# A loop over pairs of steps, with one written order for each engine, in a kernel of attention and two feed-forward layers

## The chip, the cores and the metric

One Trainium2 chip, one of its cores. The metric is the device time of one execution in microseconds (us); lower is better. The engines are PE (TensorE matmul; PEld is its weight load), DVE (VectorE), ACT (ScalarE), POOL (GpSimd) and SP (SyncE, which issues the DMAs). They run side by side, each through its own list of instructions in order, and wait for each other by semaphores.

## The reference

12,480 tokens of width 128 go through attention over 49 agents and two feed-forward layers of width 2,048:

```python
def _attn_ref(q, k, v, agents):
    a2k = sm(agents, k)                 # softmax of scaled scores
    agent_v = a2k @ v                   # 49 x 128
    q2a = sm(q, agents)                 # 12480 x 49
    return q2a @ agent_v

def _moe_ref(x, w_in, w_out):
    h = x @ w_in
    g = np.where(h >= 1, h, np.where(h <= -1, 0, (h + 1) ** 2 / 4))
    return g @ w_out

def _moe2_ref(x, w_in, w_out, s, b):
    r = np.maximum(x @ w_in, 0)
    return (s * (r * r) + b) @ w_out
```

## The kernel before

A prologue (up to some 66 us) sums keys and values into `agent_v`, turns the float64 weights into pairs of fp32r tiles (`h` for the high part, `l` for the rest), and folds `agent_v @ w_in` of the first layer into `awh` and `awl` (49 rows for the high part of the probabilities, 49 for the low, in 128 partitions).

After it the tokens are taken in 25 blocks: one of 256, 23 of 512, one of 448. A block has `JP` = 8 steps; a step is 256 of the 2,048 hidden columns, two chunks of 128, so there are `NS` = 200 steps. Step `n` of the first layer and step `m = n - 11` of the second stand side by side. The parts of a step, with the letters by which the text names them (capital for the first layer, small for the second):

- H(n), four matmuls (L581): two chunks, each with `awh` and `awl`, into a PSUM tile of two banks. h(m) (L581 too) has six: the layer's input is a pair `yh`, `yl`. These tiles, and those of the scores and the transposition, share three buffers (tag `h`); the text calls one of them a buffer.
- R(n), relu by ACT (L597), S(n), square by ACT (L603), M(n), the cap by DVE (L607), which reads the PSUM tile last and so frees it; c(n), the cast to `gh` by DVE (L618); L(n), the rest `gl` by DVE (L623). Second layer: r(m) (L599), which frees the tile; t(m), the square (L603); the cast by ACT (G, L616) or DVE (C, L618) after the pattern PAT2, by DVE alone in the last TL = 11 steps; l(m) (L623).
- O(n), six matmuls (L665) into `y`: for each chunk `wh x gh`, `wl x gh`, `wh x gl`. So the third is the first to read `gl`. o(m) is the same into `o`. O and o come two steps after their H and h.
- At a block's end yh (Y, ACT, L684) and yl (y, DVE, L687) read `y`, and Z (DVE, L691) reads `o` and stores the output.
- The probabilities of a later block: scores (q, L161), a copy by ACT (Q, L168), then ten small operations, the fillers (maximum, subtraction, Exp by ACT at L182, sum, reciprocal, product, two casts on DVE), of which `fill` takes the next at set places; then a transposition (p, L204) and its copy by ACT (P, L209).

The first 14 steps are written out in a string (`RAMP`). From step 14 on a loop over steps (L721 to L758) records the instructions: on PE in the order of `POR`, and on the other engines in that of `ORD`, one list of tokens for ACT and DVE together. The order of recording is the order on each engine. `x`, `gh` and `gl` live in rings of XB, GR and GR buffers for each layer, all 4.

Of the kernel before, what the change touches and what calls it, by code (L numbers as in the profile page):

```python
# [8 lines left out]
F32 = mybir.dt.float32  # L9
F32R = mybir.dt.float32r  # L10
# [8 lines left out]
def kernel(  # L19
# [17 lines left out]
    nc = tc.nc  # L37
    P = 128
# [37 lines left out]
    )  # L78
    WORD = "A0 A2 A1 B0 B1 C0 C1 D0 D1".split()
    PIECE = {"A0": (0, 512), "A2": (512, 512)}  # L80
    POR = "H1 QS QT O1 H2 O2".split()
    NR, ORD = 14, (
        "R1 T2 S1 Q Y G2 R2 C2 L1 F M1 y L2 F Z G1 c1"
    ).split()
    QS, QT, DX = {1: 6, 2: 7, 3: 6, 4: 4}, {2: 6, 3: 5, 4: 3}, 1
    MASK_H = 0x7FFFFE00
    WBIAS = -8.0 * 896 * 2 ** 20
    TB = 512
# [49 lines left out]

    q_t = {}
    qs_t = {}  # L140
    pt_t = {}

    def subs(t):
        w = blocks[t][1]
# [52 lines left out]
    def q_transpose(t):  # L197
        if t >= NB:
            return
        fill(len(fillers), True)  # L200
        w = blocks[t][1]
        tp = ps_h(f"tp{t}")[:, 0, :]
        for i, c0 in enumerate(subs(t)):
            nc.tensor.matmul(  # L204
                out=tp[:, c0:c0 + P], lhsT=ptok[t % NPT][:, i, :], rhs=ident_r,
                start=True, stop=True,
            )
        pt_t[t] = ptp.tile([P, TB], F32R, tag="pt", name=f"pt{t}")
# [489 lines left out]
    def ramp():  # L698
        steps = {}

        def first_q(k):
            ops = q_scores(k)
            steps[k] = [q_evac, *ops[:3], *ops[4:]]

        does = {
            "H": lambda n: H(1, n), "R": lambda n: relu(1, n), "S": lambda n: square(1, n), "M": cap,
            "g": lambda n: hi(1, n, GH(1, n) == "1"), "L": lambda n: lo(1, n), "O": lambda n: O(1, n),
            "h": lambda n: H(2, n), "r": lambda n: relu(2, n), "s": lambda n: square(2, n),
            "G": lambda n: hi(2, n, GH(2, n) == "1"), "l": lambda n: lo(2, n), "o": lambda n: O(2, n),
            "Y": lambda: evac(1, "h"), "y": lambda: evac(1, "l"),  # L710
            "u": load_q, "q": first_q, "p": q_transpose, "P": lambda n: q_evac(), "z": lambda k, i: steps[k][i](),
        }
        for token in RAMP.split():
            does[token[0]](*[int(x) for x in token[1:].split(".") if x])

    with tc.manual_schedule():
        prologue()
        late = ctx.enter_context(tc.tile_pool(name="late", bufs=1))
        ramp()
        fillers.append(lambda: nc.vector.tensor_scalar_mul(bcol, bcol, b_sb[:, 0:1]))  # L720
        for n in range(NR, NS + D + D2):  # L721
            t, j = divmod(n, JP)
            m = n - D
            a1, a2, b2 = n < NS, 0 <= m < NS, 0 <= m - 1 < NS
            b1 = 0 <= n - 1 < NS
            room[0] = 2 if n < 4 * JP else 4
            if j == 0:
                load_q(t + 2)
            for c in POR:
                if c == "H1" and a1: H(1, n)  # L730
                if c == "H2" and a2: H(2, m)
                if c == "O1" and 0 <= n - D1 < NS: O(1, n - D1)
                if c == "O2" and 0 <= m - D2 < NS: O(2, m - D2)
                if c == "QS" and j == QS.get(t, 3): fillers.extend(q_scores(t + 2))
                if c == "QT" and t > 1 and j == QT.get(t, 1): q_transpose(t + 1)
            if m == NS:
                last_step(False)
            b2 = 0 <= m - 1 < NS - 1
            a2 = 0 <= m < NS - 1
            for c in ORD:  # L740
                if c == "T2" and b2: square(2, m - 1)
                if c == "Q": q_evac()
                if c == "Y": evac(1, "h")
                if c == "y": evac(1, "l")
                if c == "Z": evac(2, "")
                if c == "G2" and b2: hi(2, m - 1, True)
                if c == "G1" and a1: hi(1, n, True)
                if c == "R1" and a1: relu(1, n)
                if c == "S1" and a1: square(1, n)
                if c == "R2" and a2: relu(2, m)  # L750
                if c == "M1" and a1: cap(n)
                if c == "c1" and a1: hi(1, n, False)
                if c == "C2" and b2: hi(2, m - 1, False)
                if c == "L1" and b1: lo(1, n - 1)
                if c == "L2" and b2: lo(2, m - 1)
                if c == "F": fill()
            if m == NS - 1:
                last_step(True)  # L758


# [33 lines left out]
```

## Time and profile before

| what | us |
|---|---|
| median of three runs (lowest, highest) | 1114.33 (1113.85, 1114.42) |
| profiled execution, its own time | 1113.61 |
| its span, first to last instruction | 1111.7 |
| PE busy | 1090.9 |
| DVE busy | 983.5 |
| ACT busy | 971.2 |

The profile follows one execution. "Busy" counts an engine's instructions; a PE that is always busy still shows its real pace only in the distance from one matmul to the next, since matmuls overlap. A row of a timeline has its start, its duration, engine, line, operation, output and inputs, and in brackets the idle time before it with what ended it. The `h` rows of both layers look alike (L581): those from `pt` are H, those from `yh` and `yl` are h.

### The profile page before, as it was taken

What the parts mean: (1) busy time and instruction counts of PE and PEld (TensorE: products, weight loads), DVE (VectorE), ACT (ScalarE), POOL (GpSimd) and SP (SyncE); (2) the same over time, 40 slices, a digit from 0 to 9 for tenths busy, and PEclk for the clock granted to TensorE, in tenths of its full rate; (3) what the DMA queues carried; (4) which work ended last, traced back from release to release, by engine and by line L of the source; (5) the groups of instructions that cost most, each with busy time, mean ns of one, the idle gap of its engine ahead of it and who ended that gap; (6) DMA issues with size and microseconds to landing.
All of it is one profiled execution on the core that took longest, in us unless ns stands there. A gap on an engine that the chain in (4) does not pass through costs nothing.

```text
span 1111.7 us, 13231 instructions
## 1 busy us (share of the span) xinstructions
PE 1090.9 (98%) x5050; PEld 879.6 (79%) x5050; DVE 983.5 (88%) x1194; ACT 971.2 (87%) x1132; POOL 0.8 (0%) x7
## 2 busy tenths in 40 slices
PE   7889999999999999999999999999999999999998
PEld 3677788888888888888888888888888888888887
DVE  8889988989889889889889899889889898898886
ACT  6889888888988988998898998998999889889886
POOL 0000000000000000000000000000000000000000
PEclk9999999999999999999999999999999999999999
DMA  9910000000000000000000000000000000000000
GB/s 352 394 58 5 15 1 20 20 1 19 19 2 19 9 11 20 0 19 20 1 19 19 1 19 19 1 20 19 1 20 20 1 19 19 1 10 10 1 10 18
DMA packets 16271, 34.82 MB, mean 31 GB/s; under 512 B 1808, under 2 KB 6736, under 8 KB 15696
## 3 DMA queue, kind: packets, MB, share of 16 engines
q1 hardware_dynamic: 16208, 33.98, 8.7%
q8 instruction: 40, 0.66, 0.2%
q14 instruction: 23, 0.19, 0.1%
HBM read 27.58 MB, written 6.39 MB: 31 GB/s over the span
## 4 chain that ended last, share of the span: by engine, by line
PE 91%; DVE 5%; ACT 1%; DMA 1%; issue 1%; SPq 0%; DVEq 0%
PE h L581 40%; PE o L665 24%; PE y L665 24%; PE qs L161 2%; DVE x L607 1%; DMA k<-in_kT 1%; PE tp L204 1%; DVE gl L623 1%; PE av L436 1%; DVE mxs L393 1%; DVE gh L618 0%; DVE wt L278 0%; ACT wt L268 0%; PE st L419 0%; DVE wu L286 0%
## 5 line engine op out<-in xcount | busy, mean ns | idle before, releaser
L623 DVE TENSOR_TENSOR gl<-x,gh 128x1024 fp32r<-128x1024 f32 (+2 forms) x399 | 475.8, 1193 | 8.0 <-ACT gh L616 0.6
L603 ACT ACTIVATE x<-x 128x1024 f32<-128x1024 f32 (+2 forms) x399 | 392.0, 1033 | 0.5
L597 ACT ACTIVATE x<-h 128x1024 f32<-128x1024 f32 (+2 forms) x200 | 201.1, 1007 | 106.8 <-PE h L581 106.4
L607 DVE SCALAR_TENSOR_TENSOR x<-h,x 128x1024 f32<-128x1024 f32 (+2 forms) x200 | 238.4, 1193 | 53.2 <-ACT x L603 50.6
L618 DVE CAST gh<-x 128x1024 fp32r<-128x1024 f32 (+2 forms) x251 | 169.7, 677 | 41.6 <-ACT x L603 41.4
L599 ACT ACTIVATE x<-h 128x1024 f32<-128x1024 f32 (+2 forms) x199 | 199.2, 1001 | 7.9 <-PE h L581 7.9
L665 PE MATMUL y<-gh,wo1h 128*128 128x512 f32 (+2 forms) x400 | 159.1, 398 | 1.7 <-DVE yl L687 1.7
L665 PE MATMUL y<-gl,wo1h 128*128 128x512 f32 (+2 forms) x400 | 156.4, 391 | 1.4 <-DVE gl L623 1.3
L581 PE MATMUL h<-pt,awh 128*128 128x512 f32 (+2 forms) x400 | 156.5, 392 | 0.7 <-ACT x L599 0.3
L665 PE MATMUL o<-gl,wo2h 128*128 128x512 f32 (+2 forms) x400 | 156.0, 390 | 0.0
L581 PE MATMUL h<-yh,wi2h 128*128 128x512 f32 (+2 forms) x400 | 155.9, 390 | 0.0
L581 PE MATMUL h<-yh,wi2l 128*128 128x512 f32 (+2 forms) x400 | 155.8, 389 | 0.0
L581 PE MATMUL h<-yl,wi2h 128*128 128x512 f32 (+2 forms) x400 | 155.8, 389 | 0.0
L665 PE MATMUL o<-gh,wo2l 128*128 128x512 f32 (+2 forms) x400 | 155.8, 389 | 0.0
L665 PE MATMUL o<-gh,wo2h 128*128 128x512 f32 (+2 forms) x400 | 155.8, 389 | 0.0
L665 PE MATMUL y<-gh,wo1l 128*128 128x512 f32 (+2 forms) x400 | 155.7, 389 | 0.0
L581 PE MATMUL h<-pt,awl 128*128 128x512 f32 (+2 forms) x400 | 155.3, 389 | 0.0
L616 ACT ACTIVATE gh<-x 128x1024 fp32r<-128x1024 f32 (+1 forms) x148 | 151.5, 1025 | 1.2 <-DVE x L607 1.2
L665 PEld LDWEIGHTS y<-gl,wo1h 128*128 128x128 f32 x400 | 75.1, 188 | 20.1 <-DVE gl L623 3.3
L581 PEld LDWEIGHTS h<-pt,awh 128*128 128x128 f32 x400 | 75.1, 188 | 18.6 <-DVE x L607 0.7
L665 PEld LDWEIGHTS y<-gh,wo1h 128*128 128x128 f32 x400 | 75.3, 188 | 17.4 <-DVE yl L687 2.6
L581 PEld LDWEIGHTS h<-yh,wi2h 128*128 128x128 f32 x400 | 75.1, 188 | 17.5 <-DVE x L607 0.4
(110 smaller groups left out, 957.1 us busy)
## 6 DMA issues: line engine op xcount, KB each, us to landing
k<-in_kT SPq DMA_DIRECT2D x12, 512.0 KB, 11.4
v<-in_v_main SPq DMA_DIRECT2D x12, 512.0 KB, 9.1
q<-in_qT SPq DMA_DIRECT2D x23, 256.0 KB, 2.7
out_T<-osb SPq DMA_DIRECT2D x23, 256.0 KB, 2.0
wu<-in_w_in SPq DMA_DIRECT2D x4, 1024.0 KB, 12.3
wu<-in_w_out SPq DMA_DIRECT2D x3, 1024.0 KB, 11.8
wu<-in_w_out SPq DMA_DIRECT2D x2, 512.0 KB, 4.8
q<-in_qT SPq DMA_DIRECT2D x1, 224.0 KB, 2.6
```

The source lines that it names most:

```text
L161: nc.tensor.matmul(out=scv[:, i, :], lhsT=qt[:, c0:c0 + P], rhs=aT, start=True, stop=True)
L204: nc.tensor.matmul(out=tp[:, c0:c0 + P], lhsT=ptok[t % NPT][:, i, :], rhs=ident_r, start=True, stop=True,)
L393: nc.vector.tensor_reduce(out=mxs[r, g:g + 1], in_=ST[r, c], op=ALU.max, axis=AX.X)
L581: nc.tensor.matmul(out=h[:, i, :w], lhsT=a[:, sl], rhs=r, start=(m == 0), stop=(m == len(ops) - 1))
L597: nc.scalar.activation(out=x, in_=h, func=ACTF.Relu, scale=0.5, bias=0.5)
L599: nc.scalar.activation(out=x, in_=h, func=ACTF.Relu)
L603: nc.scalar.activation(out=x, in_=x, func=ACTF.Square)
L607: nc.vector.scalar_tensor_tensor(out=x, in0=h, scalar=1.0, in1=x, op0=ALU.max, op1=ALU.min)
L616: nc.scalar.activation(out=a, in_=x, func=ACTF.Copy)
L618: nc.vector.tensor_copy(out=a, in_=x)
L623: nc.vector.tensor_tensor(out=b, in0=x, in1=a.bitcast(F32), op=ALU.subtract)
L665: nc.tensor.matmul(out=o[:, :w], lhsT=l[:, c, :], rhs=r[:, i, :w], start=(c == 0 and m == 0), stop=(c == KF - 1 and m == 2),)
```

## The change

- The loop over steps becomes `steady()`, over pairs of steps. For each pair it goes through three lists of tokens, one for each engine (`PAIR`; 0 and 1 behind a letter is the step of the pair), and makes of each token an operation with the keys that it depends on. Then it merges: PE's list is recorded as far as its dependencies are recorded, then ACT's, then DVE's, and again. The order on an engine is that of its own list; the fillers are taken two at each of F0 and F1 of DVE's list, and Exp lands in ACT's list where that finds it.
- Both H of a pair come first, back to back.
- `XB` falls from 4 to 3.
- The scores come at j = 7 and the transposition at j = 5 in every block (`QS`, `QT`).
- `fill_rows()` issues eight DMAs after the ramp, which copy `awh` and `awl` into two new tiles. `H1_pair` would read these, for blocks from `QB` = 99 on.

```diff
-    GR, XB, UB, WB, KV = 4, 4, 4, 2, 7
+
+    QB, RG, X1 = 99, 32, 15
+    XN = 2 * X1
+    XL = NA - XN
+
+    GR, XB, UB, WB, KV = 4, 3, 4, 2, 7
...
-    POR = "H1 QS QT O1 H2 O2".split()
-    NR, ORD = 14, (
-        "R1 T2 S1 Q Y G2 R2 C2 L1 F M1 y L2 F Z G1 c1"
-    ).split()
-    QS, QT, DX = {1: 6, 2: 7, 3: 6, 4: 4}, {2: 6, 3: 5, 4: 3}, 1
+    NR = 14
+    PAIR = {
+        "PE": "H0 h0 O0 o0 q0 O1 p1 p0 h1 q1 o1".split(),
+        "ACT": "t0 P0 Y0 R0 R1 Q0 S0 S1 G0 r0 P1 Y1 t1 r1 Q1 G1".split(),
+        "DVE": "L0 y0 C0 C1 Z1 F0 M0 M1 l0 Z0 c0 y1 c1 L1 l1 F1".split(),
+    }
+    QS, QT, DX = 7, 5, 1
...
+    def fill_rows():
+
+        extra["m"] = late.tile([P, DFF], F32R, name="awm")
+        extra["x"] = late.tile([P, DFF // 4], F32R, name="awx")
+        m, x, h, l = (w.bitcast(F32) for w in (extra["m"], extra["x"], awh, awl))
+        for i, r in enumerate((0, LO)):
+            nc.sync.dma_start(out=m[r:r + NA], in_=h[r:r + NA])
+            nc.sync.dma_start(out=m[r + NA:r + NA + X1], in_=l[i * X1:(i + 1) * X1])
+        for g in range(P // RG):
+            nc.sync.dma_start(
...
-    def fill(k=1, flush=False):
-
+    def fill(k=1):
         for _ in range(k):
-            if fillers and (flush or room[0]):
+            if fillers:
                 fillers.pop(0)()
...
+        def first(n):
+            t, j = divmod(n, JP)
+            if j == 0:
+                load_q(t + 2)
+            if t >= QB:
+                H1_pair(n)
+            else:
+                H(1, n)
+                H(1, n + 1)
...
+        for n0 in range(NR, NS + D + D2 + 2, 2):
+            for e, tokens in PAIR.items():
+                for token in tokens:
+                    c, n = token[0], n0 + int(token[1])
+                    m, j, t = n - D, n % JP, n // JP
+                    a, b = n < NS, 0 <= m < NS
...
+                    if c == "H" and a and n == n0:
+                        add(("H", n), slot(("M", n)) + slot(("M", n + 1)), first, n)
+                    elif c == "O" and n - 2 < NS:
+                        k = n - 2
+                        add(("O", k), [("L", k), ("y", k // JP - 1)], O, 1, k)
...
+                    elif c in "GC" and 0 <= m - 1 < NS - 1 and (c == "G") == (GH(2, m - 1) == "1"):
+                        add(("g", m - 1), [("t", m - 1), ("o", m - 1 - GR)], hi, 2, m - 1, c == "G")
+                    elif c == "l" and 0 <= m - 1 < NS - 1:
+                        add(("l", m - 1), [("g", m - 1), ("o", m - 1 - GR)], lo, 2, m - 1)
...
+        keys = {op[0] for ops in lists.values() for op in ops}
+        while any(lists.values()):
+            left = len(keys)
+            for ops in lists.values():
+                while ops and not any(d in keys for d in ops[0][1]):
+                    key, _, fn, args = ops.pop(0)
+                    fn(*args)
+                    keys.discard(key)
+            assert len(keys) < left
...
     with tc.manual_schedule():
         prologue()
         late = ctx.enter_context(tc.tile_pool(name="late", bufs=1))
         ramp()
+        fill_rows()
         fillers.append(lambda: nc.vector.tensor_scalar_mul(bcol, bcol, b_sb[:, 0:1]))
-        for n in range(NR, NS + D + D2):
...
+        steady()
```

Two places show what the lists move; a name has the layer, the step and a buffer number (`x1_16` is the first layer's `x` of step 16). First the head, around Exp (`qe3<-qe3`). ACT before:

```order
L616 ACTIVATE gh2_3_1094<-x2_3_1053 128x2x256
L599 ACTIVATE x2_4_1096<-h2_4_1077 128x2x256
L182 ACTIVATE qe3_1026<-qe3_1026 128x196
L597 ACTIVATE x1_16_1133<-h1_16_1109 128x1024
L603 ACTIVATE x2_4_1096<-x2_4_1096 128x2x256
```

ACT now:

```order
L670 ACTIVATE gh2_3_1110<-x2_3_1062 128x2x256
L657 ACTIVATE x2_4_1107<-x2_4_1107 128x2x256
L190 ACTIVATE qe3_1098<-qe3_1098 128x196
L651 ACTIVATE x1_16_1157<-h1_16_1122 128x1024
L651 ACTIVATE x1_17_1159<-h1_17_1127 128x1024
```

Exp stands ahead of R16 in both. What it reads is the output of DVE's subtraction (`qe3<-qe3,qm3`). DVE before, from the maximum:

```order
L178 TENSOR_REDUCE qm3_1027<-qe3_1026 128x4
L607 SCALAR_TENSOR_TENSOR x1_14_1048<-h1_14_1016,x1_14_1048 128x1024
L623 TENSOR_TENSOR gl2_2_1062<-x2_2_1008,gh2_2_1055 128x2x256
L618 CAST gh1_14_1064<-x1_14_1048 128x1024
L623 TENSOR_TENSOR gl1_14_1098<-x1_14_1048,gh1_14_1064 128x1024
L179 TENSOR_TENSOR qe3_1026<-qe3_1026,qm3_1027 128x196
L607 SCALAR_TENSOR_TENSOR x1_15_1090<-h1_15_1066,x1_15_1090 128x1024
```

DVE now, from M14:

```order
L661 SCALAR_TENSOR_TENSOR x1_14_1056<-h1_14_1026,x1_14_1056 128x1024
L661 SCALAR_TENSOR_TENSOR x1_15_1058<-h1_15_1031,x1_15_1058 128x1024
L677 TENSOR_TENSOR gl2_2_1072<-x2_2_1008,gh2_2_1067 128x2x256
L672 CAST gh1_14_1074<-x1_14_1056 128x1024
L672 CAST gh1_15_1076<-x1_15_1058 128x1024
L677 TENSOR_TENSOR gl1_14_1078<-x1_14_1056,gh1_14_1074 128x1024
L677 TENSOR_TENSOR gl2_3_1113<-x2_3_1062,gh2_3_1110 128x2x256
L186 TENSOR_REDUCE qm3_1099<-qe3_1098 128x4
L187 TENSOR_TENSOR qe3_1098<-qe3_1098,qm3_1099 128x196
```

The subtraction stood ahead of M15; now M15, c15 and l3 stand ahead of it.

The second place is the end, where the first layer is done. DVE before, in steps 200 to 203:

```order
L618 CAST gh2_189_9123<-x2_189_9092 128x1024
L687 TENSOR_TENSOR yl24_9119<-y24_8836,yh24_9118 128x448
L623 TENSOR_TENSOR gl2_189_9126<-x2_189_9092,gh2_189_9123 128x1024
L618 CAST gh2_190_9144<-x2_190_9121 128x1024
L623 TENSOR_TENSOR gl2_190_9146<-x2_190_9121,gh2_190_9144 128x1024
L618 CAST gh2_191_9164<-x2_191_9142 128x1024
L623 TENSOR_TENSOR gl2_191_9166<-x2_191_9142,gh2_191_9164 128x1024
```

DVE now:

```order
L672 CAST gh2_189_9126<-x2_189_9094 128x1024
L677 TENSOR_TENSOR gl2_188_9128<-x2_188_9087,gh2_188_9092 128x1024
L738 TENSOR_TENSOR yl24_9120<-y24_8863,yh24_9119 128x448
L677 TENSOR_TENSOR gl2_189_9131<-x2_189_9094,gh2_189_9126 128x1024
L672 CAST gh2_190_9133<-x2_190_9123 128x1024
L672 CAST gh2_191_9167<-x2_191_9161 128x1024
L677 TENSOR_TENSOR gl2_190_9169<-x2_190_9123,gh2_190_9133 128x1024
L677 TENSOR_TENSOR gl2_191_9171<-x2_191_9161,gh2_191_9167 128x1024
```

The cast of the pair's second step (189, 191) now stands ahead of `gl` of its first (188, 190). ACT's list there has `yh24` between relu and square of 189 now, and behind the square before:

```order
L653 ACTIVATE x2_189_9094<-h2_189_9074 128x1024
L735 ACTIVATE yh24_9119<-y24_8863 128x448
L657 ACTIVATE x2_189_9094<-x2_189_9094 128x1024
```

So the square of 189 comes after the last product of O199.

## Rows read from the trace of the kernel before

**Rows 1.** The page, busy time of each engine with its share of the span

```profile
PE 1090.9 (98%) x5050; PEld 879.6 (79%) x5050; DVE 983.5 (88%) x1194; ACT 971.2 (87%) x1132; POOL 0.8 (0%) x7
```

**Rows 2.** Windows: us; PE, PEld, DVE, ACT, POOL busy; clock; DMA share; GB/s

```profile
115.00:120.00 5.00, 3.25 (x19) 2.51 (x18) 4.97 (x9) 3.51 (x7) 0.00 (x0) 1.00 0.00 0
...
500.00:600.00 100.00, 100.00 (x447) 81.26 (x446) 90.05 (x107) 88.19 (x100) 0.00 (x0) 1.00 0.04 11
```

**Rows 3.** Timeline of PE, one step: first matmul of H and of h

```profile
507.15 0.40 PE L581 MATMUL h<-pt,awh 128*128 128x512 f32 x1
...
509.49 0.40 PE L581 MATMUL h<-yh,wi2h 128*128 128x512 f32 x1
```

**Rows 4.** Waits of PE's weight loads, 95 to 200 us: total, times, longest

```profile
PEld y L665 <- DVE yl L687: 2.6, 3, 2.2
PEld y L665 <- DVE gl L623: 0.4, 1, 0.4
```

**Rows 5.** Groups by line and shape: count, busy us, mean ns, idle before

```profile
L623 DVE TENSOR_TENSOR gl<-x,gh 128x1024 fp32r<-128x1024 f32 x368 | 448.8, 1220 | 7.2 <-ACT gh L616 0.6
L603 ACT ACTIVATE x<-x 128x1024 f32<-128x1024 f32 x368 | 369.5, 1054 | 0.1
L607 DVE SCALAR_TENSOR_TENSOR x<-h,x 128x1024 f32<-128x1024 f32 x184 | 224.5, 1220 | 49.4 <-ACT x L603 46.7
...
L599 ACT ACTIVATE x<-h 128x1024 f32<-128x1024 f32 x184 | 188.0, 1022 | 2.1 <-PE h L581 2.1
```

**Rows 6.** Timeline of ACT (first row) and DVE, instructions that follow each other

```profile
444.94 2.00 ACT L603 ACTIVATE x<-x 128x1024 f32<-128x1024 f32 x2
...
456.80 0.69 DVE L618 CAST gh<-x 128x1024 fp32r<-128x1024 f32 x1 [0.95 <-ACT x L603]
457.41 1.22 DVE L623 TENSOR_TENSOR gl<-x,gh 128x1024 fp32r<-128x1024 f32 x1
458.55 1.22 DVE L607 SCALAR_TENSOR_TENSOR x<-h,x 128x1024 f32<-128x1024 f32 x1
```

**Rows 7.** Timeline of DVE and ACT in the ramp: L(2), then R(5)

```profile
74.54 0.68 DVE L623 TENSOR_TENSOR gl<-x,gh 128x512 fp32r<-128x512 f32 x1
...
74.68 0.60 ACT L597 ACTIVATE x<-h 128x512 f32<-128x512 f32 x1 [0.46 <-PE h L581]
```

**Rows 8.** Timeline, head: H(14), G(13), Exp, l(3), O(16), H(20)

```profile
98.63 0.50 PE L581 MATMUL h<-pt,awh 128*128 128x512 f32 x1 [0.29 <-ACT x L599]
...
99.66 1.06 ACT L616 ACTIVATE gh<-x 128x1024 fp32r<-128x1024 f32 x1 [0.59 <-DVE x L607]
...
108.03 0.37 ACT L182 ACTIVATE qe<-qe 128x196 f32<-128x196 f32 x1
...
109.05 0.68 DVE L623 TENSOR_TENSOR gl<-x,gh 128x512 fp32r<-128x512 f32 x1
...
117.53 0.50 PE L665 MATMUL y<-gh,wo1h 128*128 128x512 f32 x1 [1.75 <-DVE yl L687]
...
124.88 0.39 PE L581 MATMUL h<-pt,awh 128*128 128x512 f32 x1
```

**Rows 9.** Timeline, tail: last matmul of O(199), yh; last of h(198), its chain

```profile
1079.61 0.36 PE L665 MATMUL y<-gl,wo1h 128*128 128x448 f32 x1
...
1080.00 0.54 ACT L684 ACTIVATE yh<-y 128x448 fp32r<-128x448 f32 x1 [0.48 <-PE y L665]
...
1101.35 0.37 PE L581 MATMUL h<-yh,wi2l 128*128 128x448 f32 x1
...
1101.76 0.92 ACT L599 ACTIVATE x<-h 128x896 f32<-128x896 f32 x1 [0.52 <-PE h L581]
...
1103.69 0.63 DVE L618 CAST gh<-x 128x896 fp32r<-128x896 f32 x1 [0.60 <-ACT x L603]
...
1104.38 0.37 PE L665 MATMUL o<-gl,wo2h 128*128 128x448 f32 x1
1104.42 1.09 DVE L623 TENSOR_TENSOR gl<-x,gh 128x896 fp32r<-128x896 f32 x1
...
1105.61 0.44 PE L665 MATMUL o<-gl,wo2h 128*128 128x448 f32 x1
```

More of the change, by code (lines that the diff above doesn't have):

```diff
@@ L140 @@
     qs_t = {}
-    pt_t = {}
+    pt_t, px_t, extra = {}, {}, {}
     def subs(t):
@@ L199, in q_transpose @@
             return
-        fill(len(fillers), True)
+        fill(len(fillers))
         w = blocks[t][1]
@@ L207, in q_transpose, with spread @@
             )
-        pt_t[t] = ptp.tile([P, TB], F32R, tag="pt", name=f"pt{t}")
-        qev.append(lambda: nc.scalar.activation(out=pt_t[t][:, :w], in_=tp[:, :w], func=ACTF.Copy))
+        pt = pt_t[t] = ptp.tile([P, TB], F32R, tag="pt", name=f"pt{t}")
+        if t >= QB:
+            px = px_t[t] = late.tile([P, TB], F32R, tag="px", name=f"px{t}", bufs=2)
+        def spread():
+            nc.scalar.activation(out=pt[:, :w], in_=tp[:, :w], func=ACTF.Copy)
+            if t < QB:
+                return
+            src = pt.bitcast(F32)
+            for i, r in enumerate((NA, LO + NA)):
+                nc.sync.dma_start(out=src[r:r + X1, :w], in_=src[i * X1:(i + 1) * X1, :w])
+            for g in range(P // RG):
+                nc.sync.dma_start(out=px.bitcast(F32)[g * RG:g * RG + XL, :w], in_=src[XN:NA, :w])
+        qev.append(spread)
     qev = []
@@ L224 @@
     XS = 2.0 ** -9 * (1 - 2.0 ** -20)
-    wu, fillers, room = {}, [], [0]
+    wu, fillers = {}, []
     def part(name):
@@ L584, in H, with H1_pair @@
         hp[layer, n] = h
+    def fill_rows():
[5 more added lines that the diff above has]
+            nc.sync.dma_start(out=m[r + NA:r + NA + X1], in_=l[i * X1:(i + 1) * X1])
+        for g in range(P // RG):
+            nc.sync.dma_start(
+                out=x[g * RG:g * RG + XL].rearrange("p (q m) -> p q m", m=P),
+                in_=l[XN:NA].rearrange("p (q g m) -> p q g m", g=4, m=P)[:, :, g, :],
+            )
+    def H1_pair(n):
+        t, j = divmod(n, JP)
+        w = blocks[t][1]
+        awm, awx = extra["m"], extra["x"]
+        out = []
+        for i in range(2):
+            hp[1, n + i] = ps_h(f"h1_{n + i}")
+            out += [hp[1, n + i][:, k, :w] for k in range(2)]
+        for g in range(4):
+            c = 2 * j + g
+            nc.tensor.matmul(
+                out=out[g], lhsT=awm[:, c * P:(c + 1) * P], rhs=pt_t[t][:, :w], start=True, stop=False
+            )
+        for g in range(4):
+            r = slice(g * RG, g * RG + XL)
+            q = slice(j // 2 * P, (j // 2 + 1) * P)
+            nc.tensor.matmul(out=out[g], lhsT=awx[r, q], rhs=px_t[t][r, :w], start=False, stop=True)
     def ring(kind, layer, n, dtype, bufs):
@@ L623, in lo @@
         nc.vector.tensor_tensor(out=b, in0=x, in1=a.bitcast(F32), op=ALU.subtract)
-        fill()
-    def fill(k=1, flush=False):
+    def fill(k=1):
         for _ in range(k):
-            if fillers and (flush or room[0]):
+            if fillers:
                 fillers.pop(0)()
-                room[0] -= 1
     def GH(layer, n):
@@ L719 @@
         ramp()
+        fill_rows()
         fillers.append(lambda: nc.vector.tensor_scalar_mul(bcol, bcol, b_sb[:, 0:1]))
-        for n in range(NR, NS + D + D2):
[L722 to L758, printed above, removed]
+        steady()
 def kernel(**inputs):
```

55 lines of the change are left out of this document (added).

## The prediction

> **What bounds the kernel now.** I read the busy shares first, then the stretches, one step of PE in order of time, PE's waits, and last the two ends of the program instruction by instruction. PE is busy for 98% of the span [rows 1], and in the middle stretch 100 of 100 us, with the clock granted in full [rows 2]. One step shows what that means: from the first product of H to the first of h stand ten products of 512 columns in 2.34 us, 0.234 us each [rows 3]; a step of 22 takes 5.13 us. DVE and ACT are at 88% and 87% [rows 1], so a step leaves each about half a microsecond. After 95 us PE waits in one place that counts: weights of y that wait 2.2 us for yl [rows 4], at the step in which block 2 begins, where the slice from 115 to 120 us shows PE at 3.25 of 5 [rows 2]. So the change can win about 2 us there and nothing in the middle; it can lose wherever one of the new lists lets PE wait.
>
> **No product goes or comes.** The branch with the packed rows asks for blocks from 99 on, and the last is 24, so every pair runs two plain H. Matmuls, evictions, squares, caps and casts keep their number and shape. The eight new DMAs of fill_rows stand on SP's queue before the load of q4. They move 1.2 MB into tiles that nothing reads; q4 is read two pairs later, over 20 us on, and SP has nothing else to do: nothing.
>
> **The middle.** I laid one pair out by hand, with 0 at its first H. PE by 0.234 us a product: H until 1.87, h0 3.27, O0 4.67, o0 6.07, O1 7.47, h1 8.87, o1 10.27. A 512-wide square or cast by ACT takes 1.05 us [rows 5] and two in a row 2.00 [rows 6], so 0.95 where the next is ready, a relu by the same overlap 0.92 (1.02 alone, [rows 5]); a gl or a cap takes 1.22 [rows 5], with the next 1.14 later, a cast's follower 0.61 later [rows 6]. ACT: R0 from 1.65, R1, S0, S1 until 5.3, G0, r0, t1, then r1, which waits for h1 until 9.1, G1, and t0 of the next pair. DVE: M0 from 4.5, M1 until 6.8, l0 7.9, c0, c1, L1 10.2, l1 (after G1) 12.2, L0 13.3. Against PE: the third product of o1 needs l0 at 9.3 (1.4 us to spare), h1 needs M0's buffer at 7.5 (1.8 to spare), the next H needs M1 (3 to spare), O1 needs L0 (3 to spare). Two pairs of a block are tighter. In one, Exp waits on ACT for two fillers behind l1, some 1.1 us, and what follows is 0.8 later: o1 keeps 0.6. In the other, o1 opens a block and needs Z0: 0.6. Rings of three for x suffice: R1 needs L of three steps back, done 2.5 us before. So the middle stays at 0.234 us a product: **nothing**, covered by 0.6 us; where that is gone, PE waits once in each of 23 blocks.
>
> **The ramp (x rings of three).** Five relus now wait for a gl of three steps back. Four of these were done in time. The fifth is R5: it ran at 74.68, and its gl ran from 74.54 for 0.68 [rows 7], so it starts 0.6 later. DVE is full up to 100 us, so some of it lasts; between 0 and 0.6 I take **+0.4**, since M5 holds DVE's queue behind it.
>
> **The head (pairs 14 to 18).** H14 starts at 98.63 in the old trace [rows 8]. Halved, the second layer's groups of block 0 (256 columns) are 0.70. New PE order: H14, H15 (until 100.6), h3, O12, o1, O13 (until 104.8). h4 takes the buffer that M14 frees. ACT has G13 from 99.66 [rows 8], then t2, R14, R15, and S14 from 103.0 to 104.05; M14 ends at 105.3: PE waits 0.55. h4, scores, o2, H16, H17, h5, O14, o3, O15 run until 113.8. Meanwhile Exp stands on ACT ahead of R16, and DVE comes to its subtraction only after M14, M15, l2, c14, c15, L14, l3 and the maximum: 105.2 + 2 x 1.14 + 0.6 (a 256-wide gl is 0.68, [rows 8]) + 2 x 0.61 + 1.14 + 0.6 + 0.6 = 110.7. In the old order Exp ran at 108.03 [rows 8] and no relu waited for it. ACT stands from 108.5 to 110.7 though H16 is ready at 108.9. R16, R17 and S16 follow, until 113.9, M16 until 115.2, whose buffer h6 takes: PE waits 1.4. M17 and l4 until 116.9: o4's third product waits 0.7. O16 and O17 find yl, L16 and L17 ready. l6 stands behind M18 and M19, until 125.8, and o6 waits 0.7. H20 starts at 126.3; with the same work behind it, it started at 124.88 [rows 8]. Waits: 0.55 + 1.4 + 0.7 + 0.7 = 3.4, less the 2.0 that went (a stop after 115.62, start at 117.53 and a slow first product [rows 8]): **+1.4**. Bounds: -2.0, if ACT gets Exp in time and all waits go; +2.5, if each wait is a third longer.
>
> **The tail (pairs 200 to 208).** Here casts of the second layer are DVE's for every step, and in DVE's new list C1, the cast of the step whose h PE has only just made, stands ahead of l0, which o1 of the same pair needs. Without first-layer work there is nothing else for PE. Full chain at 448 columns: last product of h at 1101.35, relu 1101.76, cast 1103.69 (+2.34); l0 some 0.6 behind that, 1.09 long, and the product 0.10 after its end (1104.42 + 1.09 to 1105.61) [rows 9]: +4.13. PE's own way to the third product of o1, over o0 and h1, is 1104.38 - 1101.35 = +3.03 [rows 9]. So PE waits 1.1 in pairs 206 and 208; 0.9 in 204, whose o0 is still 512 wide; in 202 the chain is 0.4 longer (relu 1.02, square 1.05, gl 1.22 [rows 5] for 0.92, 0.95 and 1.09) and PE's way 0.3: 1.2. In pair 200 ACT's new order has yh between relu and square of 189, so from the last product of O199 to o188's third: 0.39 to yh [rows 9], 0.45, square 1.10, cast 0.61, gl 1.22, 0.10, together 3.87, where PE needs 0.20 + 1.40 + 0.47 = 2.07: wait 1.8. Pair 210 has the old order again. 1.8 + 1.2 + 0.9 + 1.1 + 1.1 = **+6.1**, each a wait that nothing later gives back. Bounds: 4.9, if each of the five chains is 0.25 shorter than I read it (five starts, 0.05 each), to 7.0, if the cast's follower starts 0.75 behind it, as a dependent one does (1103.69 to 1104.42 [rows 9]).
>
> **Sum.** 0 + 0.4 + 1.4 + 6.1 = 7.9 us on the profiled execution's 1113.61, 1121.5; the median of the three runs lies 0.7 higher, so **1122.2**, 0.7% slower. By the bounds 1117.2 to 1124.4 (2.9 to 10.1 on the median). A measurement of this kernel can tell about 0.2%, 2.2 us, from no change.
>
> **A rule on the clock.** PE stood for 2.2 us before 117.53 and the slice from 115 to 120 us kept a granted clock of 1.00, the 2.4 GHz level [rows 2, 4]; no wait that I forecast is longer. The Trainium skill, "TensorE: Matmul & The Clock Gate", section "Part 1: The HAM clock gate", holds against a list that makes PE wait that half clock is the default and that idleness brings it back; this trace does not show it at such a length.
>
> **Rivals.**
> *The middle waits too* (8%). The 0.6 us of the two tight pairs come from starts of ACT and DVE that I took to 0.1 us. For: Exp's place is the one that hurts the head. Against: PE's waits push later needs back. If the chain is 0.3 past the cover, 23 x 0.3 = 7 us more: 1129.
> *Spacing falls: faster* (3%). If the 0.234 us were not PE's own but came from the order (changes of tile and of engine), eight products of H in a row, then six of h, could sit closer. It decides from 2.5 ns a product: 22 x 186 steps x 2.5 ns = 10.1 us, which pays the 7.9 and the 2.2 that can be told. At 3 ns, 12.3 less 7.9: 1110. Against: inside a group and across its border the spacing is the same [rows 3]. The same page, section "Wait — 56ns, not 53.3ns?", has back-to-back products at N / 2.4 GHz + 2.5 ns, which is 216 ns for 512 columns; by it an order could win 18 ns a product, 73 us in all; the trace's 234 ns speak against it.
> *The head gains and the tail loses little* (6%). Exp in time, -2.0, and C1 only half as late, 3: +1, 1115.3, no change. Against: the chain of the tail stands link by link in [rows 9].
> *Half clock in the tail* (3%). Five pairs of 24 products of 0.20 would take 9.7 us and not 5.9: 19 more, 1141.
>
> **Numbers.** Forecast 80%; its own range is that of the bounds, 1117.2 to 1124.4. The range given reaches from 1117 to 1126, past the upper bound for a part of the first rival. Slower: 77 of the forecast's 80 (in the other 3 the ends come out below both lower bounds), 8 and 3: 0.88. Same: 3 of the forecast and 5 of the third rival: 0.08. Faster: 3, and the 1 of the third rival in which the tail loses nothing: 0.04.
>
> **What would show it.** Right: weights of o waiting for gl once a pair from about 1085 us on, 0.9 to 1.8 us each, with the DVE cast before it waiting for ACT's square; PE busy for some 28 of the last 38 us; PE at 100 of 100 in the middle and 5.13 us a step plus scores; waits of h for a cap between 104 and 116 us, and Exp after 110 us. Wrong: PE below 100% in the middle stretches, or no waits in the tail.

## The result and the profile after it

| | median us | runs | span of the profiled execution |
|---|---|---|---|
| before | 1114.38 | 4, 1113.85 to 1115.65 | 1111.7 |
| changed | 1123.68 | 4, 1122.81 to 1124.59 | 1122.7 |

The changed kernel takes 1.0081 times as long, 95% interval 1.0068 to 1.0093: 9.3 us more. The forecast was 1122.2 in a range of 1117 to 1126, slower with 0.88.

The profiled execution of the changed kernel is the longest of its four runs (1124.59 us). Its page, and its windows (us; then PE, PEld, DVE, ACT and POOL busy; clock; DMA share; GB/s), to be set beside [rows 1, 2]:

```profile
PE 1094.9 (98%) x5050; PEld 880.9 (78%) x5050; DVE 966.1 (86%) x1194; ACT 970.0 (86%) x1132; POOL 0.9 (0%) x7
```

```profile
500.00:600.00 100.00, 100.00 (x443) 81.06 (x442) 88.45 (x108) 89.05 (x100) 0.00 (x0) 1.00 0.04 11
...
1090.00:1095.00 5.00, 4.01 (x20) 3.22 (x19) 3.50 (x4) 2.63 (x3) 0.00 (x0) 1.00 0.00 0
1095.00:1100.00 5.00, 3.24 (x16) 2.50 (x15) 2.94 (x4) 3.74 (x4) 0.00 (x0) 1.00 0.00 0
1100.00:1105.00 5.00, 5.00 (x19) 4.51 (x18) 0.94 (x2) 1.66 (x2) 0.00 (x0) 0.66 0.14 52
```

PE is busy for 100 of 100 us in the middle, as before. The time went at the two ends, where PE stood. PE's timeline in the changed kernel, every product that it idled for from H14 on, with H20 and the last product (start us, us, then the idle time before it and what ended it):

```profile
99.87 0.50 PE L602 MATMUL h<-pt,awh 128*128 128x512 f32 x1 [0.29 <-ACT x L653]
106.57 0.39 PE L602 MATMUL h<-yh,wi2h 128*128 128x256 f32 x1 [0.40 <-DVE x L661]
116.33 0.39 PE L602 MATMUL h<-yh,wi2h 128*128 128x256 f32 x1 [1.15 <-DVE x L661]
118.06 0.38 PE L716 MATMUL o<-gl,wo2h 128*128 128x256 f32 x1 [0.54 <-DVE gl L677]
126.87 0.38 PE L716 MATMUL o<-gl,wo2h 128*128 128x256 f32 x1 [0.42 <-DVE gl L677]
127.45 0.39 PE L602 MATMUL h<-pt,awh 128*128 128x512 f32 x1
...
1086.01 0.50 PE L716 MATMUL o<-gl,wo2h 128*128 128x512 f32 x1 [1.58 <-DVE gl L677]
1092.68 0.50 PE L716 MATMUL o<-gl,wo2h 128*128 128x512 f32 x1 [0.99 <-DVE gl L677]
1099.46 0.47 PE L716 MATMUL o<-gh,wo2h 128*128 128x448 f32 x1 [1.76 <-DVE osb L742]
1106.93 0.47 PE L716 MATMUL o<-gl,wo2h 128*128 128x448 f32 x1 [0.38 <-DVE gl L677]
1112.88 0.47 PE L716 MATMUL o<-gl,wo2h 128*128 128x448 f32 x1 [0.82 <-DVE gl L677]
...
1118.55 0.47 PE L716 MATMUL o<-gl,wo2h 128*128 128x448 f32 x1
```

Two marks split the 11.0 us between the two spans: the start of H14 and that of the last product (in the profile before 98.63, [rows 8], and 1107.57). A third, the y mark, is a product of y that waits for gl in the ramp. The y mark before and now, and the last product before:

```profile
75.28 0.39 PE L665 MATMUL y<-gl,wo1h 128*128 128x256 f32 x1 [0.38 <-DVE gl L623]
```

```profile
76.14 0.39 PE L716 MATMUL y<-gl,wo1h 128*128 128x256 f32 x1 [0.38 <-DVE gl L677]
```

```profile
1107.57 0.47 PE L665 MATMUL o<-gl,wo2h 128*128 128x448 f32 x1
```

H14 comes 1.24 later. Of that 0.86 lies ahead of the part of the ramp that the change touches (up to the y mark). The prologue is the same code in both, and the mark lies between 75.28 and 77.69 in the profiles of this study: it says nothing of the change. The other 0.38 is the ramp. From H14 to H20 it is 27.58 us and was 26.25: 1.33 for the head. From H14 to the last product it is 1018.68 and was 1008.94: 9.74, of which 8.4 are the tail; in between nothing is lost.

The tail's 8.4 by the starts: a gap counts from the start of the product before, less the 0.23 or 0.20 us that it would have taken, and about 0.1 more, as the product behind a wait is slow. Pair 200: 1.85; 202: 1.26; 204: 2.0; 206: 0.64; 208: 1.09. The rest is a stretch at half clock. In PE's timeline of the changed kernel nine products behind the wait of pair 204 stand 0.37 us apart, not 0.20, and the window shows the 1.2 GHz level, 0.50:

```profile
1100.83 0.58 PE L602 MATMUL h<-yh,wi2h 128*128 128x448 f32 x1
1101.20 0.58 PE L602 MATMUL h<-yl,wi2h 128*128 128x448 f32 x1
...
1104.16 0.37 PE L716 MATMUL o<-gh,wo2h 128*128 128x448 f32 x1
```

```profile
1102.00:1103.00 1.00, 1.00 (x4) 0.92 (x3) 0.00 (x0) 0.00 (x0) 0.00 (x0) 0.50 0.00 0
```

That costs 1.5 us and shortens the wait of pair 206 by 0.45 (where the clock stays full it is as long as that of 208, 1.09): 1.1 in all. Without it the tail is 7.3 and H14 to the last product 1017.6; this is the figure that the experiments are set against. Seven profiles of this study have the same tail with the same waits of 1.58, 0.99 and 1.76 us; three of them have the stretch (changed, e3, e7).

The wait of pair 204 is not the one forecast. DVE's timeline there:

```profile
1097.06 0.63 DVE L672 CAST gh<-x 128x896 fp32r<-128x896 f32 x1 [2.77 <-ACT x L657]
1097.60 1.08 DVE L677 TENSOR_TENSOR gl<-x,gh 128x896 fp32r<-128x896 f32 x1
1098.61 0.80 DVE L742 TENSOR_SCALAR osb<-o,s_sb,bcol 128x512 f32<-128x512 f32 x1
```

C1 (the cast of step 193) waits 2.77 us for its square, and l0 of 192 and then Z0 (osb of block 23) stand behind it. o1 opens block 24 there and needs the buffer that Z0 empties, so it can't even begin.

### The profile page after: what moved, and what is told of

Read it like the earlier page. It is cut to its first block, busy times and chain, and to the rows that moved or that the text cites. A ratio compares the mean times of both kernels' runs of the same rounds, so it can differ in the third digit from the quotient of the medians.

```text
span 1122.7 us, 13221 instructions
## 1 busy us (share of the span) xinstructions
PE 1094.9 (98%) x5050; PEld 880.9 (78%) x5050; DVE 966.1 (86%) x1194; ACT 970.0 (86%) x1132; POOL 0.9 (0%) x7
## 3 DMA queue, kind: packets, MB, share of 16 engines
HBM read 27.58 MB, written 6.39 MB: 30 GB/s over the span
## 4 chain that ended last, share of the span: by engine, by line
PE 89%; DVE 6%; ACT 2%; issue 1%; DMA 1%; SPq 0%; DVEq 0%; ACTq 0%
PE h L602 38%; PE o L716 24%; PE y L716 23%; PE qs L169 2%; DVE gl L677 2%; DVE x L661 1%; DMA k<-in_kT 1%; PE tp L212 1%; DVE gh L672 1%; ACT x L657 1%; PE av L457 1%; ACT x L651 1%; DVE mxs L414 0%; DVE wt L299 0%; PE st L440 0%
## 5 line engine op out<-in xcount | busy, mean ns | idle before, releaser
L677 DVE TENSOR_TENSOR gl<-x,gh 128x1024 fp32r<-128x1024 f32 (+2 forms) x399 | 470.8, 1192 | 35.7 <-ACT gh L670 32.9
L657 ACT ACTIVATE x<-x 128x1024 f32<-128x1024 f32 (+2 forms) x399 | 405.0, 1045 | 1.9
L661 DVE SCALAR_TENSOR_TENSOR x<-h,x 128x1024 f32<-128x1024 f32 (+2 forms) x200 | 230.4, 1192 | 84.9 <-ACT x L657 84.8
L653 ACT ACTIVATE x<-h 128x1024 f32<-128x1024 f32 (+2 forms) x199 | 201.9, 1014 | 81.1 <-PE h L602 79.9
L651 ACT ACTIVATE x<-h 128x1024 f32<-128x1024 f32 (+2 forms) x200 | 190.2, 1006 | 1.6 <-DVE gl L677 1.2
L672 DVE CAST gh<-x 128x1024 fp32r<-128x1024 f32 (+2 forms) x251 | 163.5, 675 | 16.4 <-ACT x L657 16.3
L716 PE MATMUL y<-gh,wo1h 128*128 128x512 f32 (+2 forms) x400 | 156.0, 390 | 0.0
L716 PEld LDWEIGHTS o<-gl,wo2h 128*128 128x128 f32 x400 | 75.3, 188 | 23.8 <-DVE gl L677 6.8
```

What stands on the lines that cost most here:

```text
L651: nc.scalar.activation(out=x, in_=h, func=ACTF.Relu, scale=0.5, bias=0.5)
L653: nc.scalar.activation(out=x, in_=h, func=ACTF.Relu)
L661: nc.vector.scalar_tensor_tensor(out=x, in0=h, scalar=1.0, in1=x, op0=ALU.max, op1=ALU.min)
L672: nc.vector.tensor_copy(out=a, in_=x)
L716: nc.tensor.matmul(out=o[:, :w], lhsT=l[:, c, :], rhs=r[:, i, :w], start=(c == 0 and m == 0), stop=(c == KF - 1 and m == 2),)
```

## The experiments

| run | edit to the changed kernel | median us | ratio to before, 95% interval | y mark to H14 | H14 to last product |
|---|---|---|---|---|---|
| before | | 1114.36 to 1114.74 | | 23.35 | 1008.94 |
| changed | | 1123.68 | 1.0068 to 1.0093 | 23.73 | 1018.68, 1017.6 at full clock |
| e1_tail | lists from pair 200 on | 1115.79 | 0.9999 to 1.0017 | 23.74 | 1010.31 |
| e2_head | Exp later in pair 16 | 1120.97 | 1.0046 to 1.0071 | 23.69 | 1015.59 |
| e3_xb4 | rings of four, no copies | 1123.93 | 1.0074 to 1.0102 | 23.37 | 1018.62, with the half clock |
| e4_packed | packed products | 1098.22 | 0.9840 to 0.9867 | 23.69 | 992.05 |
| e5_osb_first | Z0, Y1 in the tail | 1120.97 | 1.0043 to 1.0073 | 23.69 | 1014.86 |
| e6_cover_512 | 512 columns behind Exp | 1125.90 | 1.0086 to 1.0120 | 23.74 | 1018.99 |
| e7_cover_1024 | 1024 columns behind Exp | 1135.48 | 1.0172 to 1.0203 | 23.75 | 1029.62, with the half clock |
| e8_best | e4, e1, e2, rings of four | 1088.36 | 0.9749 to 0.9778 | 23.43 | 982.77 |
| e9_best_late_exp | e8, Exp later everywhere | 1087.18 | 0.9742 to 0.9770 | 23.38 | 981.15 |
| e10_best_qb2 | e9, packed from block 2 | 1095.55 | 0.9818 to 0.9846 | 30.52 | 981.66 |
| e11_cover_late_exp | e7, Exp later everywhere | 1133.74 | 1.0158 to 1.0187 | 23.68 | 1027.40 |

The kernel before was run beside each group of them. The last two columns are read in one profile each; they leave the prologue out and tell tenths.

**The tail** (e1_tail, e5_osb_first). The lists are replaced from pair 200 on: ACT's in both runs, DVE's by the first of the two in e1 and by the second in e5 (written short):

```diff
+ if e == "ACT" and n0 >= 200: "t0 P0 Y0 R0 R1 Q0 S0 S1 G0 r0 P1 t1 Y1 r1 Q1 G1"
+ if e == "DVE" and n0 >= 200:
+     "L0 y0 C0 l0 Z0 F0 M0 M1 C1 c0 y1 c1 L1 l1 F1"
+     "L0 y0 C0 Z0 C1 F0 M0 M1 l0 c0 y1 c1 L1 l1 F1"
```

> Only the last pairs differ from the changed kernel: from pair 200 on DVE's list has l0 and Z0 ahead of C1, and ACT's has Y1 behind t1. Theory: the queue order alone made the five waits of the tail (gaps of PE of 1.85, 1.26, 2.0, 0.64 and 1.09 us in the profile of the changed kernel, 6.8 in all), and the stretch at half clock (nine products at 0.37 us for 0.20, 1.5 us) came only with them. Then PE runs through from 1080 us to its last product as in the kernel before, and the run is 8.3 us shorter than the changed kernel's profiled one and 6.8 shorter than its runs without the half-clock stretch: about 1116 us. Rival: something else is late next (Z0 behind l0, yl behind the cast); then one or two waits of 0.5 to 1 stay and it gains 5 to 6. Rival: the pairs themselves and not the lists' tail are the cost; then it gains under 2.

H14 to the last product fell by 7.3 from the full-clock figure (1017.6 to 1010.31), all of the tail. Its windows, against those of the changed kernel above:

```profile
1090.00:1095.00 5.00, 5.00 (x25) 4.30 (x24) 3.68 (x5) 3.74 (x5) 0.00 (x0) 1.00 0.00 0
1095.00:1100.00 5.00, 5.00 (x26) 4.61 (x25) 4.12 (x5) 3.70 (x5) 0.00 (x0) 1.00 0.14 52
```

No product waits and the clock stays full. So the loss was in the order of these queues alone: neither pairs as such nor a wait next in line. What is left to the kernel before, 1.37 us, is the head.

> As the changed kernel, but from pair 200 on Z0 stands ahead of C1 in DVE's list (l0 stays behind C1), and ACT's list has Y1 behind t1. It takes the wait of pair 204 apart. Theory: two things held o1 there, one behind the other: the product of l0 behind the cast C1, as in the other pairs, and osb behind l0, which the forecast left out. With osb done early, o1 of pair 204 starts in time and its third product waits for gl alone: a gap of 0.9 to 1.0 us in place of 2.0. In pair 200 the wait falls from 1.85 to 1.4, as yh no longer stands between relu and square. Pairs 202, 206, 208 keep theirs. So 1.4 us less, and the half-clock stretch, which came behind the wait of pair 204, should be seen less often. Rival: osb is not the cause and the chain of h193 is; then the gap stays at 2.0.

PE's timeline in pairs 202 and 204 of it; the last two rows are the second and the third product of o1 in pair 204:

```profile
1091.67 0.50 PE L716 MATMUL o<-gl,wo2h 128*128 128x512 f32 x1 [0.99 <-DVE gl L677]
...
1096.74 0.37 PE L716 MATMUL o<-gh,wo2l 128*128 128x448 f32 x1
1097.93 0.47 PE L716 MATMUL o<-gl,wo2h 128*128 128x448 f32 x1 [0.82 <-DVE gl L677]
```

With osb done early, o1 of pair 204 begins in time and its third product waits as in 206 and 208: 1.19 - 0.20 = 0.99, and 0.1 for the slow product. That is what the forecast had for this pair; the other 0.9 was osb. In pair 200 the expectation fell: no wait is left there, not 1.4. I had taken Y1 for its own 0.45 us, but it held the square until PE was through O199; behind t1, the square of 189 starts 0.03 us after its relu ends and the whole 1.85 goes. Both together: 2.7 less.

**The head** (e2_head). In pair 16 alone F0 stands behind M1: `"L0 y0 C0 C1 Z1 M0 M1 F0 l0 Z0 c0 y1 c1 L1 l1 F1"`.

> Only pair 16 differs from the changed kernel: the fillers F0 stand behind M1 in DVE's list, so that Exp comes behind the squares of 16, 17 and 5 on ACT. Theory: ACT stood 2.1 us for DVE's subtraction with R16 behind it; without that M16 starts where DVE has done its gl of step 15, at 113.0 and not 115.05 us, the wait of h6 (1.15 us of PE) goes and that of the product of o4 behind it (0.54) shrinks to 0.1; the waits of h4 (0.40) and o6 (0.42) stay. So 1.2 to 1.9 us less, 1.5 taken. Rival: DVE is behind by itself, Exp or no Exp; then M16 moves by less than 0.5 and the gain is under 0.5.

ACT around Exp, first the changed kernel (square of 4, Exp, R16 and R17), then e2:

```profile
109.14 0.62 ACT L657 ACTIVATE x<-x 128x512 f32<-128x512 f32 x1
111.88 0.37 ACT L190 ACTIVATE qe<-qe 128x196 f32<-128x196 f32 x1 [2.11 <-DVE qe L187]
112.15 1.92 ACT L651 ACTIVATE x<-h 128x1024 f32<-128x1024 f32 x2
```

```profile
110.45 0.62 ACT L657 ACTIVATE x<-x 128x512 f32<-128x512 f32 x1
111.40 1.96 ACT L651 ACTIVATE x<-h 128x1024 f32<-128x1024 f32 x2 [0.33 <-PE h L602]
...
117.55 0.36 ACT L190 ACTIVATE qe<-qe 128x196 f32<-128x196 f32 x1
```

R16 now waits for its own product. The waits of h6 (1.15) and of o4 (0.54) are gone, those of h4 and o6 stay, as expected. H14 to H20 is 25.63, 1.95 less than in the changed kernel and 0.6 less than before the change; I had 1.5, and at most 1.9, as I took the idle times of the two waits; by the starts (as in the tail) they are 1.41 and 0.79.

**The ramp** (e3_xb4). `GR, XB, ... = 4, 4, ...`, and the call of fill_rows taken out.

> Differs from the changed kernel in two things: the rings of x have four buffers again, and the eight copies into the unused tiles are gone. Theory: R5 no longer waits for the gl of step 2, H14 comes 0.4 us earlier against the first product of y, and nothing else moves: 0.4 us less; the copies cost nothing. Rival: rings of three also bind in the steady loop, or the copies delay a load: then more than 1 us less. Rival: the 0.4 is taken back by DVE, which is full there: no difference. Differences of this size can be told in the profile only.

The relu of step 5, first in the changed kernel, then in e3:

```profile
76.17 0.60 ACT L651 ACTIVATE x<-h 128x512 f32<-128x512 f32 x1 [0.99 <-DVE gl L677]
```

```profile
75.32 0.60 ACT L651 ACTIVATE x<-h 128x512 f32<-128x512 f32 x1 [0.47 <-PE h L602]
```

With four buffers it waits for its product again, as before the change [rows 7]. The y mark to H14 is 23.37 against 23.73, the rest unchanged: 0.36, and the copies cost nothing where they stand. The run changes two things; that the 0.36 belongs to the rings is told by the relu, which no longer waits for a gl. The medians can't tell it.

**The cover in the middle** (e6, e7, e11). The forecast rested on 0.6 us of cover in two pairs of a block. The changed kernel's trace has both: in the pair of Exp the gl that o1's third product reads ends at 581.33, 0.59 ahead of it, and where o1 opens a block osb ends 0.57 ahead of it:

```profile
580.11 1.22 DVE L677 TENSOR_TENSOR gl<-x,gh 128x1024 fp32r<-128x1024 f32 x1
...
581.92 0.40 PE L716 MATMUL o<-gl,wo2h 128*128 128x512 f32 x1
```

```profile
558.66 0.81 DVE L742 TENSOR_SCALAR osb<-o,s_sb,bcol 128x512 f32<-128x512 f32 x1
...
560.04 0.39 PE L716 MATMUL o<-gh,wo2h 128*128 128x512 f32 x1
```

A copy behind Exp eats it (written short; it stands in 21 blocks, from block 4 on):

```diff
  nc.scalar.activation(out=ev, in_=ev, func=ACTF.Exp, ...)
+ nc.scalar.activation(out=spare, in_=wi2h[:, :512], func=ACTF.Copy)
```

> As the changed kernel, with one more instruction on ACT behind Exp in each of 21 blocks: a copy of 512 columns into a tile that nothing reads, 0.60 us alone, some 0.5 in a row. It tests the cover of 0.6 us in the middle (in the profile of the changed kernel the gl of Exp's pair ends 0.59 us ahead of its product). Theory: 0.5 later is still covered; no change, within 0.5 us. Rival: the cover is thinner, or DVE's fillers that read Exp come late too; then up to 21 x 0.3 = 6 us more.

> The same with 1024 columns, 1.05 us alone and some 0.95 in a row. Theory: 0.95 less the cover of 0.59 is a wait of o1 for gl of 0.36, and 0.1 for the slow product behind a wait, in 21 blocks: 8 to 10 us more. Rival: the next pair takes the delay up, as ACT idles over 1 us in it; it does, but only behind o1, so this theory gives no change only if o1 does not need that gl; then 0.

The weights of that product, first with 512, then with 1024 columns:

```profile
582.80 0.19 PEld L716 LDWEIGHTS o<-gl,wo2h 128*128 128x128 f32 x1 [0.25 <-DVE gl L677]
```

```profile
586.48 0.19 PEld L716 LDWEIGHTS o<-gl,wo2h 128*128 128x128 f32 x1 [0.56 <-DVE gl L677]
```

With 512 columns (0.52 later) the product starts on time, but its weights wait 0.25 and it is slow by 0.07: 1.4 us over 21 blocks, where I expected none. With 1024 columns (0.95 later) H14 to the product that waits in pair 200 (1095.67 us), ahead of its half-clock stretch, is 996.62 us, where the changed kernel has 986.14: 10.5 more, or 0.50 a block. 0.40 of that lies at the product of o1, the expected mechanism, and the rest at h1, whose weights wait for a cap; the whole is a little above the expected 8 to 10. (The stretch costs this run 1.6 us: it ends earlier than in the changed kernel and shortens no later wait. The 10.9 that e11's expectation starts from took it at 1.05.) So the cover was as large as forecast, but not free to its last 0.1, as weights that load late cost too.

> The changed kernel with the copy of 1024 columns behind Exp, and with F0 behind M1 in all pairs below 200, so that Exp and the copy stand on ACT behind the squares and the yh of their pair and not ahead of its relus. It tests whether it is Exp's place that makes that pair the tight one. Theory: the copy's 0.95 now falls where nothing is due soon; of the 10.9 us that it cost (without the half-clock stretch of that profile) 0 to 1 are left, and the head is 1.95 faster as in the run that moved Exp in pair 16: 1121 to 1123 us. Rival: ACT at 89 of 100 has no 0.95 to spare in any pair of a block; then 5 us or more of the 10.9 stay.

Here the theory fell. H14 to the last product is 1027.40; with 1.95 given back by the head that is 11.75 above 1017.6, more than e7's 10.5. ACT runs without a pause from 583.5 us over the copy to the relus and squares of the next pair, and it is that pair's o1 that waits:

```profile
595.87 0.50 PE L716 MATMUL o<-gl,wo2h 128*128 128x512 f32 x1 [0.30 <-DVE gl L677]
```

So it isn't Exp's place alone. With ACT at 89 of 100 the next pair too has no 0.95 us to spare, and the rival (5 us or more stay) holds.

**The branch that is never entered** (e4_packed): `QB, RG, X1 = 3, 32, 15` in place of 99.

> The branch that the changed kernel carries and never enters is entered from block 3 on (QB = 3): each of 88 pairs makes its four chunks of the first layer with four products over all 128 rows and four products over 19 rows each, in four row groups of 32, in place of eight. Theory: the four short products run beside each other; the first layer of a pair takes 5 x 0.234 = 1.17 us of PE and not 1.87, 0.70 x 88 = 62 us at most. DVE and ACT, at 88 and 89 of 100 us in the middle, would be at 95 and 96 then, so PE begins to wait for them, and 25 to 55 us are gained. Rival: the four run one after the other, 0.234 us each; then it is 8 products as before and the time within 2 us of the changed kernel. Rival: going over to row groups and back stops PE's overlap of products twice a pair; then slower, by 88 x 0.2 to 0.4 us, 18 to 35.

One pair's first layer on PE and the first product of h behind it, packed (x4 is a group of four):

```profile
549.79 1.09 PE L632 MATMUL h<-pt,awm 128*128 128x512 f32 x4
550.80 0.51 PE L638 MATMUL h<-px,awx 19*128 19x512 f32 x4
551.24 0.51 PE L602 MATMUL h<-yh,wi2h 128*128 128x512 f32 x1
551.59 0.39 PE L602 MATMUL h<-yl,wi2h 128*128 128x512 f32 x1
```

The four products over 19 rows take 0.51 us together, where four in a row would take 4 x 0.234 = 0.94: they run beside each other. From the first product to the second of h it is 1.80 us. The same two in the changed kernel:

```profile
550.73 0.39 PE L602 MATMUL h<-pt,awh 128*128 128x512 f32 x1
...
552.82 0.40 PE L602 MATMUL h<-yl,wi2h 128*128 128x512 f32 x1
```

That is 2.09, so 0.29 a pair, 25.5 us over 88 pairs, and H14 to the last product fell by 25.5. That is 41% of the 62 at most. DVE and ACT, at 90 and 91 of 100, took little of the rest: PE is at 100 of 100 in the middle still, and of short waits of its weights e9 below gets 1.6 us back. The packed group costs 0.44 and not one product's 0.23, it starts 0.07 late, and the product behind it is followed 0.12 late. The Trainium skill, "TensorEngine Tiling (Array Packing)", section "Key Properties", says that tiles work independently and that a change of mode drains the engine; these rows agree, with 0.2 us a pair for going there and back.

**Together** (e8, e9, e10). e8: QB = 3, the lists of e1 and e2, rings of four. e9: F0 behind M1 in every pair below 200. e10: QB = 2 and fill_rows ahead of the ramp.

> All that helped, together: the packed products of the first layer from block 3 on, the lists of the tail and of pair 16 of the two earlier runs, and rings of x of four. Theory: the parts lie in stretches of their own and add up: from 1098.2 us 7.2 of the tail, 1.6 of the head and 0.4 of the ramp go, to 1089 us, some 25 us below the kernel before. Rival: with PE 0.30 us shorter a pair the cover in the middle is 0.3, and anything moved there shows; then 1090 to 1095.

> The best version with Exp's place changed in every block, not in pair 16 alone: F0 behind M1 in DVE's list of all pairs below 200. In the best version weights of o wait 0.2 us for a gl in each of 21 blocks, in the pair in which Exp holds up the relus. Theory: the cover of that pair grows by what ACT stands for DVE's subtraction, 1.0 us, so these 21 waits go; a product behind such a wait costs some 0.07, so 1.5 us less than 1088.4. Rival: Exp now delays the second layer's relu behind it, and the wait moves there: no change or slower.

> The run before it with the packed products from block 2 on and the copies of the packed weights ahead of the ramp on SP's queue. Theory: four pairs more at 0.30 us, 1.2 less. Rival: in those pairs, 16 to 22, DVE sets the pace (the waits of h4 and o6 for cap and gl, 0.4 each, come back larger): under 0.5 less. Rival: the rows of pt of block 2, copied at the end of the ramp, or the copies of the weights land late: slower by some us at H16.

e8 comes to 1088.36 where the parts summed to 1089. In e9 the 21 waits of o's weights for gl (5.1 us in all in e8) are gone, and H14 to the last product falls by 1.6 for an expected 1.5: 1087.18 us, 2.4% below the kernel before, with an interval of 2.3 to 2.6%. e10 is 8.4 us slower than e9, by the second rival, but for the most part in another place than I thought. SP's queue in e10, then the scores of block 2 and a packed product of H16:

```profile
69.08 0.91 SPq L613 DMA_DIRECT2D awm<-awh  x1
...
81.60 2.08 SPq L160 DMA_DIRECT2D q<-in_qT  x2
```

```profile
87.74 1.91 PE L169 MATMUL qs<-a,q 128*128 128x49 f32 x8 [5.30 <-DMA q<-in_qT]
...
118.52 0.50 PE L638 MATMUL h<-px,awx 19*128 19x512 f32 x1 [0.52 <-DMA px<-pt]
```

In e10 the eight copies hold SP from 69.08 to 81.60, 12.5 us, with the load of q2 behind them, and the scores of block 2 stand for it. In the changed kernel the copies are recorded behind the ramp, but SP runs them at about the same time; there the load of q3 stands ahead of them and that of q4 behind:

```profile
69.03 0.33 SPq L160 DMA_DIRECT2D q<-in_qT  x1
69.59 0.90 SPq L613 DMA_DIRECT2D awm<-awh  x1
...
83.25 1.68 SPq L160 DMA_DIRECT2D q<-in_qT  x1
```

Nothing that stands behind them is due, so their 13.7 us (69.59 to 83.25) cost nothing. From H14 on the packed products of block 2 gain nothing either (981.66): H16 waits 0.52 us for the copied rows of pt, as the second rival had it, and the next two pairs take as long as in e9 (from H18 to H20 8.83 us for 8.81, from H20 to H22 10.04 for 9.99). The first rival would have that, but its larger waits are not there (o6 waits 0.41, and 0.42 in e9), so what takes the gain stays open.

## Why the prediction was right, and where it was off

- **Middle, 0:** right. PE is at 100 of 100, and the two tight pairs keep 0.59 and 0.57 us, as laid out by hand.
- **Ramp, +0.4:** 0.38, from R5 behind the gl of step 2; e3 takes it back. R5 itself is 0.62 later against the y mark, as forecast (0.6). How much of it would last was a choice between 0 and 0.6, and that it hit so closely is luck.
- **Head, +1.4:** 1.33. The four waits are where they were put, and by the starts, as in the tail, each has its size: h4 0.67 for 0.55, h6 1.41 for 1.4, o4 0.79 for 0.7, o6 0.69 for 0.7 (the brackets of the rows above give the idle time alone). They sum to 3.56, and 2.01 went: 1.55, so 0.2 came back in gaps that I did not trace. Exp came at 111.88, or 110.64 with H14 put where the forecast had it, for 110.7. The sum printed there does not give 110.7, though: its terms add up to 111.6, because it starts at 105.2, the end of M14, and counts M14 again; from M14's start they give 110.5. That Exp is the cause, e2 shows for h6 and o4; for h4 and o6 it stays a reading of the traces.
- **Tail, +6.1:** 7.3 at full clock. Four of five terms are within 0.1: 1.85 for 1.8, 1.26 for 1.2, 1.09 for 1.1 twice. The step that failed is "0.9 in 204, whose o0 is still 512 wide": 2.0. I costed o1's wait for l0 there and left out that o1 opens block 24 and needs Z0, which stands behind C1 and l0 in the same list. I had named that need for the middle, where it is covered, and not asked for it again where the cover is gone. e5 shows the 0.9 that was right and the rest as osb's. e1 shows that the lists alone made the five waits. PE is busy for 29.1 of the last 38 us, for some 28 forecast. The 7.3 lies above the tail's own bounds, 4.9 to 7.0 (by the 0.75 that they name, the upper one is 6.1 + 5 x 0.15 = 6.85); the whole stayed in its range because the bounds of the head were wide.
- **Sum, 7.9:** 0.38 + 1.33 + 7.3 = 9.0, and 1.1 more in the profiled execution for the half clock; the medians differ by 9.3.
- **"No wait that I forecast is longer"** than 2.2 us, so no half clock: it came in the profiled execution all the same, behind three waits of 1 to 1.8 us within 15, and cost 1.1 us and not the rival's 19, as it lasted nine products. The length of the longest wait was the wrong measure. The sentence cited against the change was nearer than I made it: the Trainium skill, "TensorE: Matmul & The Clock Gate", section "Part 1: The HAM clock gate", has idleness bring half clock back, and this trace agrees in so far as the granted clock of 0.50 stands right behind those waits. Why four of seven profiles with the same waits kept the full clock, no run here settles.
- **Rivals.** Spacing (3%): out, a plain step's products stay 0.23 us apart. The middle waits too: out, but near, as e6 finds the edge at 0.5 us. The head gains and the tail loses little: out, with 1.33 and 7.3.

## What to carry to other kernels

When a list of queue orders is written for the steady state, walk its first and its last steps by hand: there the engine it feeds has no other work, and an entry one place too early (C1 ahead of l0, Y1 ahead of t1, Exp ahead of a relu) cost its whole wait here. For each consumer at such a place, list everything it needs, its output buffer too, and not only the one input that was late last time. And look what a change prepares and leaves off: the packed branch, off by one constant, was worth 25 us where the order around it cost 9.

## What was unexpected in the hardware

Four products over 19 rows, each in its own group of 32 rows and into its own half of an h, took 0.51 us together, with some 0.2 us for going over and back. A product whose weights came 0.25 us late started in time and was still 0.07 us slow (e6); one behind a wait was some 0.1 slow. The same three waits were followed by half clock for 3.3 us in three profiles and not in four. And a queue that looks free by its few transfers can be held long by them: eight copies between tiles held SP for 12.5 us in e10 and 13.7 in the changed kernel, and what they cost hung on the load behind them.
